# A routed expert kernel whose head is reordered: loads in one queue, weights in small staged pieces

## The chip, the cores and the metric

The kernel runs on one core of one Trainium2 chip. The metric is device microseconds of one execution; each figure is the median of several runs. A few names: PE is the matrix engine, DVE the vector engine, ACT the scalar engine, POOL the GpSimd engine, SP the sync engine, which here only issues transfers. "SPq" and "ACTq" in a row are transfers being issued by SP or ACT.

## The reference: what is computed

```python
# x: (8, 3584, 192), weight: (8, 7); 28672 tokens in all
w = softmax(weight)                                   # per head, over 7 taps
out[b,s,h,:] = sum_k w[h,k] * x_pad[b, s+k, h, :]     # causal conv, 8 heads of 24 channels
...
logits = x @ w_gate                                   # 8 experts
e_idx  = argmax(logits);  gate_w = softmax(logits)[e_idx]
eom    = sigmoid(x @ w_output_gate)
h  = relu(x[mask] @ w1[e])                            # 192 -> 1024
out[mask] = gate_w * eom[:, e] * (h @ w2[e])          # 1024 -> 192
```

## The kernel before, in words

The 28672 tokens are cut into 16 units of 1792 (16 blocks of 112). For each unit a generator `front(u)` does eight convolution matmuls, one for each head, against a banded matrix `band`; each result goes from PSUM to `cv`. Then come six groups of PE transposes (`tt`), the routing matmul (`pl`, `lt`), a transpose back (`pg`, `gb`), the argmax and softmax on DVE with two Exp instructions on ACT (`ex` and `ogs`), a running count for each expert (`pk`, `R`), and the scaled rows `xrow`. POOL then writes the unit's rows into a DRAM stream sorted by expert (`xcg_sorted`), in 16 indirect transfers. Two units make enough rows for the first four expert slots of 512 tokens. A slot is read back from the stream by two transposing transfers (`xa`, `xb`), multiplied by w1 (`first`) and w2 (`second`), and written out by four indirect transfers on POOL.

The program order on each engine is the order of the Python code, and every engine works through its own list in that order. The part up to the first slot is called the head here. It loads the units 0 and 1 (`load_x`), builds `band` from the conv weights by way of a DRAM scratch (`conv_band`), writes 512 rows of zeros at the start of each expert's part of the stream (the "guard"), loads all weights of 8 experts as fp32 and casts them to fp16 in the resident tile `wres` (`load_w`, `cast_w`), and runs `front(0)` and `front(1)`. The units 2 and 3 are loaded from inside `front(0)` and `front(1)`, after the eight convolutions of each, because `xt` has two buffers.

In the head before, ACT issues the band, the gate weights and the 32 guard transfers of 64 KB each. The weights of one expert come in four transfers into three staging buffers: `sa` (128x1024), `sb` (64x1024), and two halves of w2 (128x768). Two casts of an expert run on ACT and two on DVE. `evac` gives the copies from PSUM to the two engines in turn. One expert's casts and the next expert's loads follow each fifth step of the fronts:

```python
    while live:
        live = drain(f0, 1)
        emit_in(2)
        k += 1
        if k % 5 == 0:
            drain(wgen, 1)
```

At most eight transfers issued by SP and ACT together are under way at a time: there are eight completion semaphores for them, used in turn, and the issue of a transfer waits until the one eight places earlier has landed.

Of the kernel before, what the change touches and what calls it, by code (L numbers as in the profile page):

```python
# [11 lines left out]
FP16 = mybir.dt.float16  # L12
FP32 = mybir.dt.float32
# [8 lines left out]
def kernel(  # L22
# [10 lines left out]
    nc = tc.nc  # L33

    B, S, D = x.shape
    H, KW = weight.shape
    E = moe_w1.shape[0]
    F = moe_w1.shape[2]
# [3 lines left out]
    BT = 112  # L42
# [6 lines left out]
    TT = 512  # L49
    CAP = TT + N  # L50
    FCH = F // 128
    RW = 256
    IDC = 192
    ZW = 2 * BT + PADL + 2
    WE = F + F + FCH * D
    BIG = float(1 << 30)

    x_nd = x.rearrange("b s d -> (b s) d")
    xcg = nc.dram_tensor("xcg_sorted", (E * CAP, RW), FP16, kind="Internal").ap()
    z_dram = nc.dram_tensor("conv_band", (H, ZW), FP32, kind="Internal").ap()  # L60

    const = ctx.enter_context(tc.tile_pool(name="const", bufs=1))
    wst = ctx.enter_context(tc.tile_pool(name="wst", bufs=3))
    px = ctx.enter_context(tc.tile_pool(name="px", bufs=2))
    pcv = ctx.enter_context(tc.tile_pool(name="pcv", bufs=2))
    pct = ctx.enter_context(tc.tile_pool(name="pct", bufs=1))
# [11 lines left out]
    def load_x(u):  # L78
        xt = px.tile([128, NB, D], FP32, tag="xt", name="xt")
        t0 = u * UT  # L80

        def src(c0, nblk, q0, q1):
            return bass.AP(tensor=x_nd.tensor,
                           offset=x_nd.offset + (t0 + c0 * BT - PADL + q0) * D,
                           ap=[[D, q1 - q0], [BT * D, nblk], [1, D]])
        c0 = 0
        if u % UPB == 0:
            c0 = 1
            nc.vector.memset(xt[0:PADL, 0:1, :], 0.0)
            nc.sync.dma_start(xt[PADL:KI, 0:1, :], src(0, 1, PADL, KI))  # L90
        nc.sync.dma_start(xt[0:BT, c0:NB, :], src(c0, NB - c0, 0, BT))
        nc.sync.dma_start(xt[BT:KI, c0:NB, :], src(c0, NB - c0, BT, KI))
        return xt


    zt = const.tile([H, ZW], FP32)
    nc.vector.memset(zt, 0.0)
    cw = const.tile([H, KW], FP32)
    nc.sync.dma_start(cw, weight)
    xts = {0: load_x(0)}  # L100
    xts[1] = load_x(1)
    cmx = const.tile([H, 1], FP32)
    nc.vector.tensor_reduce(out=cmx, in_=cw, axis=AX.X, op=ALU.max)
    nc.vector.tensor_scalar(out=cw, in0=cw, scalar1=cmx, scalar2=None, op0=ALU.subtract)
# [3 lines left out]
    nc.vector.reciprocal(out=csm, in_=csm)  # L108
    nc.vector.tensor_scalar(out=zt[:, BT - 1:BT - 1 + KW], in0=cw, scalar1=csm,
                            scalar2=None, op0=ALU.mult)  # L110
    nc.scalar.dma_start(out=z_dram, in_=zt)
    band = const.tile([128, H, BT], FP32)
    for p0, p1 in ((0, BT), (BT, KI)):
        nc.scalar.dma_start(band[p0:p1],
                            bass.AP(tensor=z_dram.tensor, offset=z_dram.offset + p0,
                                    ap=[[1, p1 - p0], [ZW, H], [1, BT]]))


    wg = const.tile([128, 4, 32], FP32)
    nc.vector.memset(wg, 0.0)  # L120
    for i, (p0, p1, d0) in enumerate([(0, 128, 0), (0, 64, 128), (64, 128, 0), (0, 128, 64)]):
        nc.scalar.dma_start(wg[p0:p1, i, 0:E], moe_w_gate[d0:d0 + p1 - p0, :])
        nc.scalar.dma_start(wg[p0:p1, i, E:2 * E], moe_w_output_gate[d0:d0 + p1 - p0, :])


    ones_t = const.tile([128, 128], FP32)
# [48 lines left out]
    NXR = 3  # L175
    xrows = [const.tile([128, NB, RW], FP16, name=f"xrow{i}") for i in range(NXR)]
    for xr in xrows:
        nc.gpsimd.memset(xr[:, :, IDC:RW], 0.0)
        nc.vector.tensor_copy(out=xr[:, :, IDC + 1], in_=idlf)


# [1 line left out]
    for m in msks:  # L183
        nc.vector.memset(m, 0.0)


    zrow = const.tile([128, RW], FP16)
    nc.vector.memset(zrow, 0.0)


    wres = const.tile([128, E * WE], FP16)
    nc.gpsimd.memset(
        bass.AP(tensor=wres.tensor, offset=wres[64:65, F:F + 1].offset,
                ap=[[wres.ap[0][0], 64], [WE, E], [1, F]]), 0.0)

    def load_w(e):
        sa = wst.tile([128, F], FP32, tag="w", name="sa")
        nc.sync.dma_start(sa, moe_w1[e, 0:128, :])
        sb = wst.tile([128, F], FP32, tag="w", name="sb")
        nc.sync.dma_start(sb[0:64], moe_w1[e, 128:D, :])  # L200
        w2v = moe_w2[e].rearrange("(p c) d -> p c d", c=FCH)
        s2 = []
        for i in range(2):
            t = wst.tile([128, F], FP32, tag="w", name="s2")
            nc.sync.dma_start(t[:, 0:4 * D].rearrange("p (c d) -> p c d", d=D),
                              w2v[:, 4 * i:4 * i + 4, :])
            s2.append(t)
        return sa, sb, s2

    def cast_w(e, st):  # L210
        sa, sb, s2 = st
        o = e * WE
        nc.scalar.copy(out=wres[:, o:o + F].rearrange("p (c j) -> p c j", c=FCH),
                       in_=sa.rearrange("p (j c) -> p c j", c=FCH))
        nc.vector.tensor_copy(
            out=wres[0:64, o + F:o + 2 * F].rearrange("p (c j) -> p c j", c=FCH),
            in_=sb[0:64].rearrange("p (j c) -> p c j", c=FCH))
        nc.scalar.copy(out=wres[:, o + 2 * F:o + 2 * F + 4 * D], in_=s2[0][:, 0:4 * D])
        nc.vector.tensor_copy(out=wres[:, o + 2 * F + 4 * D:o + WE], in_=s2[1][:, 0:4 * D])

    sync_flip = [0]

    def evac(o, i):
        sync_flip[0] ^= 1
        if sync_flip[0]:
            nc.scalar.copy(out=o, in_=i)  # L226
        else:
            nc.vector.tensor_copy(out=o, in_=i)  # L228


    def front(u):
# [14 lines left out]
        for g in range(6):  # L246
            pt = ps_f.tile([128, 512], FP32, tag="pf", name="pt")
            for j in range(4):
                m, i = (g // 3) * 4 + j, g % 3
# [6 lines left out]
        pl = ps_f.tile([128, 512], FP32, tag="pf", name="pl")  # L256
# [4 lines left out]
                                 tt[:, g // 2 + i, (g % 2) * 4 * BT:(g % 2 + 1) * 4 * BT],  # L261
                                 start=(i == 0), stop=(i == 1), tile_position=(0, 32 * g))
        lt = pct.tile([128, 4 * BT], FP32, tag="lt", name="lt")
        nc.scalar.copy(out=lt, in_=pl[:, 0:4 * BT])
        yield
        pg = ps_f.tile([128, 512], FP32, tag="pf", name="pg")
        for j in range(4):
# [5 lines left out]
            out=gb[0:BT],  # L273
            in_=pg[0:BT].rearrange("p (k e) -> p k e", e=32)[:, :, 0:16])
# [12 lines left out]
            out=sc[P], in0=dl[P], scalar=0.0,  # L287
# [43 lines left out]
        xr = xrows[u % NXR]  # L331
# [5 lines left out]
        for g in range(4):  # L337
            nc.vector.tensor_tensor(  # L338
                out=xrv[P, g // 2, g % 2, :, 0:D], in0=cvv[P, g // 2, g % 2],
# [15 lines left out]
    def emit_in(n=1):  # L355
        while n and pend:
            if last[0] == "in":
                nc.gpsimd.nop()
            pend.popleft()()
            last[0] = "in"  # L360
            n -= 1
# [4 lines left out]
    def nodep(i, group, others):  # L366
        inst = i.ins if hasattr(i, "ins") else i
        for o in others:
            tc.declare_no_dep(inst, group=o, reason="distinct rows of the stream or output")
        tc.add_to_no_dep_group(group, inst)  # L370
# [5 lines left out]
    def plan_half(hf, nm):  # L376
# [18 lines left out]
        iu = pr.tile([128, EH, 4], U32, tag=f"iu{nm}", name="iu", bufs=3)  # L395
        nc.vector.tensor_scalar(out=iu, in0=iv, scalar1=BIG, scalar2=None, op0=ALU.mult)
        return [(e0 + i, bu[0:1, i:i + 1], iu[:, i, :]) for i in range(EH)]
# [19 lines left out]
    def w_at(off):  # L417
        return lambda o, n: wres[:, off + o:off + o + n]
# [64 lines left out]


    for e in range(E):
        for g in range(TT // 128):
            i = nc.scalar.dma_start(out=xcg[e * CAP + g * 128:e * CAP + (g + 1) * 128, :],
                                    in_=zrow)
            nodep(i, "guard", ())

    def drain(g, n=None):
        k = 0
        while n is None or k < n:
            try:
                next(g)
            except StopIteration:
                return False
            k += 1
        return True

    def chain(*gs):
        for g in gs:
            yield from g

    staged = {0: load_w(0)}

    def weights():
        for e in range(E):
            cast_w(e, staged.pop(e))
            if e + 1 < E:  # L510
                staged[e + 1] = load_w(e + 1)
            yield

    f0 = chain(front(0), front(1))
    wgen = weights()
    live = True
    k = 0
    while live:
        live = drain(f0, 1)
        emit_in(2)  # L520
        k += 1
        if k % 5 == 0:
            drain(wgen, 1)
    drain(wgen)
    emit_in(len(pend))

    prev = None
    for u in range(1, NU):
        todo = []
# [9 lines left out]
        for e, inv, xab in todo:  # L539
            s = Slot(xab, w_at(e * WE), inv)  # L540
            for q in range(4):
# [30 lines left out]
    with tc.For_i(0, rn, 1):  # L572
# [9 lines left out]
        sel = pr.tile([128, 1], U32, tag="sel", name="sel")  # L582
        nc.vector.tensor_scalar(out=sel, in0=om, scalar1=-float(WE), scalar2=float(E * WE),
                                op0=ALU.mult, op1=ALU.add)
# [16 lines left out]
        iv1 = pr.tile([128, 4], FP32, tag="iv1", name="iv1")  # L601
        nc.vector.tensor_scalar(out=iv1, in0=rowf, scalar1=tk1, scalar2=BIG,
                                op0=ALU.is_lt, op1=ALU.mult)
# [39 lines left out]
```

## Time and profile before

| | |
|---|---|
| median of 3 runs | 858.84 us (858.24 to 859.68) |
| the profiled execution, its time | 857.44 us |
| its span in the profile | 855.7 us |
| first expert matmul | 149.03 us |
| mean granted TensorE clock | 0.904 |
| busy: PE, DVE, ACT, POOL | 622.6, 334.0, 345.7, 523.7 us |

The span is the time from the first to the last recorded instruction; the execution's own time is 1.7 us longer. Busy shares are a mean over a head, in which the engines mostly wait, and a long main part that repeats for each unit.

### The profile page before, as it was taken

Reading aid. Unit: us, or ns where it says so; the run is one execution under the profiler, and the core shown is the slowest. Engines: PE = TensorE matmul, PEld = TensorE weight load, DVE = VectorE, ACT = ScalarE, POOL = GpSimd, SP = SyncE. Lnnn points to the kernel's source line nnn. Section 1 sums busy time; section 2 is a strip of 40 time slices with the busy share of each in tenths; the row PEclk is TensorE's granted clock in tenths of the full one; section 3 lists DMA queues with packets and bytes.
Section 4 is the critical chain, followed back from the end, with each engine's and each line's share of the span. In section 5 each row is a group of like instructions: output and inputs, shape, how many; then the busy total and the mean of one; then the engine's idle time right before and its main releaser. Section 6 shows DMA issues by size and latency. Waiting matters only on the chain. (4 is left out here: it accounts for less than half of the span.)

```text
span 855.7 us, 12810 instructions
## 1 busy us (share of the span) xinstructions
PE 622.6 (73%) x4612; PEld 397.9 (46%) x4612; DVE 334.0 (39%) x843; ACT 345.7 (40%) x503; POOL 523.7 (61%) x529
## 2 busy tenths in 40 slices
PE   1343610878098898989898989797979898669963
PEld 0121300435056565656555656464656555446641
DVE  6025340355035445362626253535353535112230
ACT  0133310325035454545444545454544544346631
POOL 4003415004775777777777777777777777777751
PEclk9975555889589999999999999999999999979987
DMA  7586741421263444444444445363632323244110
GB/s 163 162 200 185 215 102 51 105 68 31 62 156 102 124 106 126 113 118 117 119 109 131 106 126 139 101 140 95 147 90 77 84 78 91 70 108 124 59 38 6
DMA packets 132695, 92.93 MB, mean 109 GB/s; under 512 B 83379, under 2 KB 121428, under 8 KB 132631
## 3 DMA queue, kind: packets, MB, share of 16 engines
q1 hardware_dynamic: 105472, 52.81, 26.2%
q0 software_dynamic: 20672, 36.75, 14.6%
q10 hardware_dynamic: 6486, 2.55, 1.2%
q8 instruction: 36, 0.59, 0.3%
q14 instruction: 29, 0.23, 0.1%
HBM read 36.19 MB, written 42.34 MB: 92 GB/s over the span
## 5 line engine op out<-in xcount | busy, mean ns | idle before, releaser
L471 POOL DMA_INDIRECT out_dram<-y,oi x260 | 262.1, 1008 | 153.9 <-issue 71.4
L349 POOL DMA_INDIRECT xcg_sorted<-xrow,du x256 | 251.0, 980 | 165.8 <-DVE xrow L338 89.0
L442 ACT ACTIVATE ht<-pp 128x1024 f16<-128x1024 f32 x195 | 199.5, 1024 | 216.6 <-PE pp L436 192.8
L434 PE MATMUL pp<-xa,wres 128*128 128x512 f16 x520 | 201.1, 387 | 90.8 <-DMA xa<-xcg_sorted 64.7
L453 PE MATMUL pyt<-wres,ht 128*128 128x192 f16 (+1 forms) x2080 | 220.7, 249 | 22.4 <-DVE ht L440 22.4
L453 PEld LDWEIGHTS <-ht 128*128 128x128 f16 x2080 | 180.7, 99 | 82.5 <-DVE ht L440 25.7
L436 PE MATMUL pp<-xb,wres 128*128 128x512 f16 x520 | 200.9, 386 | 2.3 <-DMA xb<-xcg_sorted 2.3
L236 PE MATMUL pc<-xt,band 118*112 118x384 f32 x256 | 110.5, 560 | 46.8 <-DMA wg<-in_moe_w_gate_dram 18.1
L464 ACT COPY y<-pyt 128x384 f32<-128x384 f32 x130 | 62.1, 478 | 104.3 <-PE pyt L453 49.7
L436 PEld LDWEIGHTS <-wres 128*128 128x128 f16 (+1 forms) x520 | 51.4, 99 | 107.0 <-issue 77.1
L440 DVE TENSOR_SCALAR ht<-pp 128x1024 f16<-128x1024 f32 x65 | 79.4, 1221 | 46.5 <-PE pp L436 45.1
L228 DVE COPY cv<-pc 112x384 f32<-112x384 f32 x64 | 35.5, 556 | 146.0 <-PE pc L236 145.9
L236 PEld LDWEIGHTS pc<-xt,band 118*112 118x112 f32 x256 | 47.6, 199 | 85.9 <-ACT cv L226 24.9
L434 PEld LDWEIGHTS <-wres 128*128 128x128 f16 (+1 forms) x520 | 51.2, 98 | 64.7 <-DMA xa<-xcg_sorted 21.1
L467 DVE CAST oi<-pyt 128x4 uint32<-128x4 f32 x65 | 10.4, 160 | 180.9 <-ACT y L464 169.5
L226 ACT COPY cv<-pc 112x384 f32<-112x384 f32 x64 | 30.3, 476 | 76.8 <-PE pc L236 42.8
L250 PE MATMUL pt<-identf,cv 112*128 112x112 f32 x384 | 49.7, 273 | 12.4 <-ACT tt L226 6.6
L338 DVE TENSOR_TENSOR xrow<-cv,gs 112x768 f16<-112x768 f32 x64 | 58.3, 954 | 0.0
L250 PEld LDWEIGHTS pt<-identf,cv 112*128 112x128 f32 x384 | 41.9, 147 | 24.7 <-ACT tt L226 10.6
L228 DVE COPY tt<-pt 128x448 f32<-128x448 f32 x48 | 29.7, 621 | 34.3 <-PE pt L250 34.3
L226 ACT COPY tt<-pt 128x448 f32<-128x448 f32 x48 | 25.5, 530 | 32.4 <-PE pt L250 32.4
L259 PE MATMUL pl<-tt,wg 128*32 128x448 f32 x256 | 32.2, 596 | 2.0 <-ACT tt L226 1.0
(101 smaller groups left out, 284.2 us busy)
## 6 DMA issues: line engine op xcount, KB each, us to landing
xt<-in_x_dram SPq DMA_DIRECT2D x8, 1344.0 KB
xt<-in_x_dram SPq DMA_DIRECT2D x8, 1260.0 KB
s<-in_moe_w_dram SPq DMA_DIRECT2D x16, 384.0 KB
out_dram<-y,oi POOLq DMA_INDIRECT x260
sa<-in_moe_w_dram SPq DMA_DIRECT2D x8, 512.0 KB
xcg_sorted<-xrow,du POOLq DMA_INDIRECT x256
xcg_sorted<-zrow ACTq DMA_DIRECT2D x32, 64.0 KB
sb<-in_moe_w_dram SPq DMA_DIRECT2D x8, 256.0 KB
```

The source lines that it names most:

```text
L228: nc.vector.tensor_copy(out=o, in_=i)
L236: nc.tensor.matmul(pc[0:BT, 0:NB * GH], band[0:KI, h, :], xt[0:KI, :, h * GH:(h + 1) * GH], start=True, stop=True)
L250: nc.tensor.matmul(pt[:, j * BT:(j + 1) * BT], cvf[0:BT, m * 2 * D + i * 128:m * 2 * D + (i + 1) * 128], identf[0:BT, 0:BT], is_transpose= ...
L338: nc.vector.tensor_tensor(out=xrv[P, g // 2, g % 2, :, 0:D], in0=cvv[P, g // 2, g % 2], in1=gs[P, g:NB:4].unsqueeze(2).to_broadcast([BT, 4 ...
L349: i = nc.gpsimd.indirect_dma_start(out=xcg, out_offset=bass.IndirectOffsetOnAxis(ap=du[0:BT, kc(c):kc(c) + 1], axis=0), in_=xr[0:BT, c, :] ...
L434: nc.tensor.matmul(pp[:, j, :], self.w(fc * 128, 128), self.xa, start=True, stop=False)
L436: nc.tensor.matmul(pp[:, j, :], self.w(F + fc * 128, 128), self.xb, start=False, stop=True)
L440: nc.vector.tensor_relu(out=ht, in_=pp)
L442: nc.scalar.activation(out=ht, in_=pp, func=AF.Relu)
L453: nc.tensor.matmul(self.pp[:, o:o + D], self.ht[fc // 2][:, fc % 2, q * 128:(q + 1) * 128], self.w(2 * F + fc * D, D), start=(fc == 0 and ...
L464: nc.scalar.copy(out=self.y[:, q - 1:q + 1, :], in_=self.pp[:, 0:2 * D].rearrange("p (g d) -> p g d", d=D))
L471: i = nc.gpsimd.indirect_dma_start(out=out, out_offset=bass.IndirectOffsetOnAxis(ap=self.oi[:, j:j + 1], axis=0), in_=self.y[:, j, :], in_ ...
```

## The change

The same data is computed. Six things differ, all ahead of the main part but one:

- On SP's queue the order is now: unit 0, the conv scratch and the band, the gate weights, unit 1, the guard, then weights. ACT issues one transfer only, the conv weights.
- The guard is 8 transfers of 256 KB, with four stream rows for each partition, on SP.
- The weights come in 48 pieces of 256 KB (six for each expert) into five staging buffers; a new piece is loaded whenever one has been cast. All casts are on ACT: two of 128x512 and two of 64x512 with a strided read, three of 128x512 that are contiguous, for each expert.
- Each step of the fronts is followed by one piece's cast, in place of an expert's casts each fifth step.
- While the head lasts (`fill[0]`), every copy from PSUM is on DVE; afterwards they alternate again. `lt` now counts among the copies that alternate.
- The clears of `xrow` and `wres` move from POOL to DVE; those of `wres` cover the same bytes.

```diff
-    nc.sync.dma_start(cw, weight)
+    nc.scalar.dma_start(cw, weight)
     xts = {0: load_x(0)}
-    xts[1] = load_x(1)
...
-    nc.scalar.dma_start(out=z_dram, in_=zt)
+    nc.sync.dma_start(out=z_dram, in_=zt)
...
-        nc.scalar.dma_start(band[p0:p1],
+        nc.sync.dma_start(band[p0:p1],
...
+    xts[1] = load_x(1)
...
-        nc.gpsimd.memset(xr[:, :, IDC:RW], 0.0)
+        nc.vector.memset(xr[:, :, IDC + 2:RW], 0.0)
...
+    def load_w(e, i):
+
+        t = wst.tile([128, FH], FP32, tag="w", name="ws")
+        if i < 2:
+            nc.sync.dma_start(t, moe_w1[e, 0:128, i * FH:(i + 1) * FH])
+        elif i == 2:
+            for k in range(2):
+                nc.sync.dma_start(t[64 * k:64 * k + 64],
+                                  moe_w1[e, 128:D, k * FH:(k + 1) * FH])
+        else:
+            w2v = moe_w2[e].rearrange("(p c) d -> p (c d)", c=FCH)
+            nc.sync.dma_start(t, w2v[:, (i - 3) * FH:(i - 2) * FH])
+        return t
...
     def evac(o, i):
         sync_flip[0] ^= 1
-        if sync_flip[0]:
+        if sync_flip[0] and not fill[0]:
             nc.scalar.copy(out=o, in_=i)
...
-        nc.scalar.copy(out=lt, in_=pl[:, 0:4 * BT])
+        evac(lt, pl[:, 0:4 * BT])
...
-        for g in range(TT // 128):
-            i = nc.scalar.dma_start(out=xcg[e * CAP + g * 128:e * CAP + (g + 1) * 128, :],
-                                    in_=zrow)
-            nodep(i, "guard", ())
+        i = nc.sync.dma_start(
+            out=xcg[e * CAP:e * CAP + TT, :].rearrange("(p g) w -> p (g w)", g=GR), in_=zrow)
+        nodep(i, "guard", ())
...
     def weights():
-        for e in range(E):
-            cast_w(e, staged.pop(e))
-            if e + 1 < E:
-                staged[e + 1] = load_w(e + 1)
+        todo = [(e, i) for e in range(E) for i in range(NWP)]
+        ld = deque()
+        for k, (e, i) in enumerate(todo):
+            while len(ld) < NWST and k + len(ld) < len(todo):
+                ld.append(load_w(*todo[k + len(ld)]))
+            cast_w(e, ld.popleft(), i)
             yield
...
-        k += 1
-        if k % 5 == 0:
-            drain(wgen, 1)
+        drain(wgen, 1)
```

ACT before, from its last gate-weight transfer to the first Exp of unit 0 (`zrow` is the guard's source, `cv`, `tt` and `lt` are copies from PSUM, `sa` and `s` are staged weights):

```order
L123 DMA wg<-in_moe_w_output_gate_dram 128x8
L487 DMA xcg_sorted<-zrow 128x256 x32
L226 COPY cv<-pc 112x16x24 x3
L213 CAST wres<-sa 128x1024
L218 CAST wres<-s_216 128x768
L226 COPY cv<-pc 112x16x24
L226 COPY tt<-pt 128x448
L213 CAST wres<-sa 128x1024
L218 CAST wres<-s_244 128x768
```

ACT with the change, from its first weight cast to the two Exps of unit 0 (`ws` is a staged piece):

```order
L220 CAST wres<-ws 128x8x64 x2
L225 CAST wres<-ws 64x8x64 x2
L230 CAST wres<-ws 128x512 x3
L220 CAST wres<-ws 128x8x64 x2
L225 CAST wres<-ws 64x8x64 x2
L230 CAST wres<-ws 128x512 x3
L220 CAST wres<-ws 128x8x64 x2
L225 CAST wres<-ws 64x8x64 x2
L230 CAST wres<-ws 128x512
L298 ACTIVATE ex<-dl 112x128
L230 CAST wres<-ws 128x512
L323 ACTIVATE ogs<-ogs 112x16
```

The guard transfers and the copies from PSUM have left ACT. Ahead of unit 0's `ex` now stand the casts of 17 pieces, and ahead of unit 1's `ex`, by the same count further down the list, those of 40.

SP with the change, from the gate weights to the third expert's first pieces:

```order
L123 DMA wg<-in_moe_w_output_gate_dram 128x8
L92 DMA xt<-in_x_dram 112x16x192
L93 DMA xt<-in_x_dram 6x16x192
L500 DMA xcg_sorted<-zrow 128x1024 x8
L206 DMA ws<-in_moe_w_dram 128x512 x2
L209 DMA ws<-in_moe_w_dram 64x512 x2
L213 DMA ws<-in_moe_w_dram 128x512 x3
L206 DMA ws<-in_moe_w_dram 128x512 x2
L209 DMA ws<-in_moe_w_dram 64x512 x2
L213 DMA ws<-in_moe_w_dram 128x512 x3
L91 DMA xt<-in_x_dram 112x192
L92 DMA xt<-in_x_dram 112x15x192
```

The weights stand behind unit 1 and the whole guard, and unit 2 is requested after 12 pieces (unit 3, by the same list, after 36). Before, SP's first weight load came right after unit 1, and the guard went out beside it on ACT's queue.

DVE with the change, from the clear of the guard's source to unit 0's first wait on an Exp (`sm` reads `ex`):

```order
L191 MEMSET zrow 128x512
L195 MEMSET wres 64x8x512
L242 COPY cv<-pc 112x16x24 x8
L90 MEMSET xt 6x192
L242 COPY tt<-pt 128x448 x6
L242 COPY lt<-pl 128x448
L286 COPY gb<-pg 112x256
L292 TENSOR_REDUCE mx<-gb 112x16
...
L322 TENSOR_REDUCE ogs<-og 112x16
L325 TENSOR_REDUCE sm<-ex 112x16
```

No weight cast stands between these any more; before, each unit's copies had four to six of DVE's weight casts among them.

## Rows read from the trace of the kernel before

**Rows 1.** Busy time by stretch: PE, PEld, DVE, ACT, POOL, clock, DMA share, GB/s

```profile
0.00:149.00 149.00, 43.40 (x154) 19.84 (x155) 49.63 (x108) 31.75 (x38) 43.88 (x45) 0.70 0.60 154
149.00:235.00 86.00, 51.43 (x327) 29.31 (x327) 31.52 (x83) 23.63 (x38) 26.66 (x28) 0.82 0.27 68
235.00:835.00 600.00, 521.42 (x4088) 344.93 (x4087) 251.29 (x649) 287.41 (x423) 449.20 (x453) 0.97 0.42 107
```

**Rows 2.** Timeline, end of the head: start, duration, engine, line, instruction, [idle before]

```profile
120.10 0.28 DVE L311 TENSOR_REDUCE sm<-ex 112x16 f32<-112x128 f32 x1
...
124.47 1.40 POOL L349 DMA_INDIRECT xcg_sorted<-xrow,du  x1 [25.62 <-DVE xrow L338]
...
144.11 0.94 POOL L349 DMA_INDIRECT xcg_sorted<-xrow,du  x1 [0.30 <-issue]
...
149.03 0.59 PE L434 MATMUL pp<-xa,wres 128*128 128x512 f16 x1 [36.84 <-DMA xa<-xcg_sorted]
...
200.12 1.00 POOL L471 DMA_INDIRECT out_dram<-y,oi  x1 [55.07 <-ACT ht L442]
```

**Rows 3.** Timeline of ACT and its issues, around the guard

```profile
19.69 17.04 ACTq L487 DMA_DIRECT2D xcg_sorted<-zrow  x32
36.77 0.86 ACT L226 COPY cv<-pc 112x384 f32<-112x384 f32 x2 [33.96 <-DMA xcg_sorted<-zrow]
```

**Rows 4.** Groups by line and shape, first 150 us: busy, mean ns, idle before

```profile
L213 ACT CAST wres<-sa 128x1024 f16<-128x1024 f32 x8 | 16.3, 2036 | 15.6 <-DMA sa<-in_moe_w_dram 15.6
...
L218 ACT CAST wres<-s 128x768 f16<-128x768 f32 x8 | 6.6, 831 | 0.2 <-DMA s<-in_moe_w_dram 0.2
L219 DVE CAST wres<-s 128x768 f16<-128x768 f32 x8 | 4.5, 563 | 26.1 <-DMA s<-in_moe_w_dram 26.1
L228 DVE COPY cv<-pc 112x384 f32<-112x384 f32 x8 | 4.4, 552 | 24.5 <-PE pc L236 24.4
```

**Rows 5.** Timeline: first casts of three experts, and the last expert's

```profile
71.14 2.03 ACT L213 CAST wres<-sa 128x1024 f16<-128x1024 f32 x1
...
98.88 2.06 ACT L213 CAST wres<-sa 128x1024 f16<-128x1024 f32 x1
...
114.00 2.03 ACT L213 CAST wres<-sa 128x1024 f16<-128x1024 f32 x1 [3.72 <-DMA sa<-in_moe_w_dram]
...
119.10 0.56 DVE L219 CAST wres<-s 128x768 f16<-128x768 f32 x1 [3.07 <-DMA s<-in_moe_w_dram]
```

**Rows 6.** Busy time by stretch, columns as in rows 1

```profile
2.00:17.00 15.00, 0.00 (x0) 0.00 (x0) 12.44 (x25) 0.29 (x2) 10.39 (x9) 1.00 1.03 216
...
32.00:37.00 5.00, 0.00 (x0) 0.00 (x0) 0.00 (x0) 0.23 (x1) 0.00 (x0) 1.00 0.47 141
...
94.00:97.00 3.00, 0.31 (x2) 0.34 (x3) 1.03 (x2) 0.00 (x0) 2.21 (x3) 0.58 1.02 368
104.00:109.00 5.00, 4.15 (x12) 0.87 (x6) 1.23 (x3) 0.53 (x1) 0.00 (x0) 0.50 1.13 261
```

**Rows 7.** Timeline, start: band, unit 1's second transfer, first convolution

```profile
11.54 0.84 ACTq L114 DMA_DIRECT2D band<-conv_band  x2
...
17.81 0.28 SPq L92 DMA_DIRECT2D xt<-in_x_dram  x1
...
18.12 2.87 PE L236 MATMUL pc<-xt,band 118*112 118x384 f32 x4 [18.12 <-DMA wg<-in_moe_w_gate_dram]
```

**Rows 8.** Timeline of PE in unit 1's front (a conv matmul counts twice)

```profile
86.82 4.18 PE L236 MATMUL pc<-xt,band 118*112 118x384 f32 x6 [1.65 <-DVE cv L228]
...
96.69 4.43 PE L250 MATMUL pt<-identf,cv 112*128 112x112 f32 x20 [5.21 <-DVE cv L228]
102.16 4.89 PE L259 MATMUL pl<-tt,wg 128*32 128x448 f32 x16 [1.03 <-ACT tt L226]
```

**Rows 9.** Timeline: the clear on POOL, and a DVE instruction beside it

```profile
7.30 6.92 POOL L192 MEMSET wres<- 64x8192 f16 x1
7.31 6.94 DVE L143 TENSOR_SCALAR rev<-eoff 128x8 f32<-128x8 f32 x1
```

More of the change, by code (lines that the diff above doesn't have):

```diff
@@ L55 @@
     WE = F + F + FCH * D
+    NWST = 5
     BIG = float(1 << 30)
@@ L62 @@
     const = ctx.enter_context(tc.tile_pool(name="const", bufs=1))
-    wst = ctx.enter_context(tc.tile_pool(name="wst", bufs=3))
+    wst = ctx.enter_context(tc.tile_pool(name="wst", bufs=NWST))
     px = ctx.enter_context(tc.tile_pool(name="px", bufs=2))
@@ L121 @@
     for i, (p0, p1, d0) in enumerate([(0, 128, 0), (0, 64, 128), (64, 128, 0), (0, 128, 64)]):
-        nc.scalar.dma_start(wg[p0:p1, i, 0:E], moe_w_gate[d0:d0 + p1 - p0, :])
-        nc.scalar.dma_start(wg[p0:p1, i, E:2 * E], moe_w_output_gate[d0:d0 + p1 - p0, :])
+        nc.sync.dma_start(wg[p0:p1, i, 0:E], moe_w_gate[d0:d0 + p1 - p0, :])
+        nc.sync.dma_start(wg[p0:p1, i, E:2 * E], moe_w_output_gate[d0:d0 + p1 - p0, :])
+    xts[1] = load_x(1)
     ones_t = const.tile([128, 128], FP32)
@@ L184 @@
         nc.vector.memset(m, 0.0)
-    zrow = const.tile([128, RW], FP16)
+    GR = TT // 128
+    zrow = const.tile([128, GR * RW], FP16)
     nc.vector.memset(zrow, 0.0)
     wres = const.tile([128, E * WE], FP16)
-    nc.gpsimd.memset(
+    nc.vector.memset(
         bass.AP(tensor=wres.tensor, offset=wres[64:65, F:F + 1].offset,
                 ap=[[wres.ap[0][0], 64], [WE, E], [1, F]]), 0.0)
[L196 to L208, printed above, removed]
@@ L210, in cast_w @@
-    def cast_w(e, st):
-        sa, sb, s2 = st
-        o = e * WE
[L213 to L219, printed above, removed]
+    FH = F // 2
@@ new lines @@
+    NWP = 6
+    def load_w(e, i):
[10 more added lines that the diff above has]
+        return t
@@ new lines, in cast_w @@
+    def cast_w(e, t, i):
+        o = e * WE
+        if i < 2:
+            nc.scalar.copy(
+                out=wres[:, o:o + F].rearrange("p (c j) -> p c j", c=FCH)[:, :, i * 64:i * 64 + 64],
+                in_=t.rearrange("p (j c) -> p c j", c=FCH))
+        elif i == 2:
+            for k in range(2):
+                nc.scalar.copy(
+                    out=wres[0:64, o + F:o + 2 * F].rearrange(
+                        "p (c j) -> p c j", c=FCH)[:, :, k * 64:k * 64 + 64],
+                    in_=t[64 * k:64 * k + 64].rearrange("p (j c) -> p c j", c=FCH))
+        else:
+            nc.scalar.copy(out=wres[:, o + 2 * F + (i - 3) * FH:o + 2 * F + (i - 2) * FH],
+                           in_=t)
@@ L221 @@
     sync_flip = [0]
+    fill = [True]
     def evac(o, i):
         sync_flip[0] ^= 1
-        if sync_flip[0]:
+        if sync_flip[0] and not fill[0]:
             nc.scalar.copy(out=o, in_=i)
@@ L503, in chain @@
             yield from g
-    staged = {0: load_w(0)}
     def weights():
-        for e in range(E):
-            cast_w(e, staged.pop(e))
-            if e + 1 < E:
-                staged[e + 1] = load_w(e + 1)
+        todo = [(e, i) for e in range(E) for i in range(NWP)]
[4 more added lines that the diff above has]
+            cast_w(e, ld.popleft(), i)
             yield
@@ L516 @@
     live = True
-    k = 0
     while live:
@@ L520 @@
         emit_in(2)
-        k += 1
-        if k % 5 == 0:
-            drain(wgen, 1)
+        drain(wgen, 1)
     drain(wgen)
     emit_in(len(pend))
+    fill[0] = False
     prev = None
```

## The prediction

> **What bounds the kernel now.** I read the busy time by stretch first, because the page's shares mix two stages. In the main part, 235 to 835 us, POOL issues 453 indirect transfers in 600 us [rows 1]. When nothing holds it back, a scatter takes 0.94 us with 0.30 us of issue ahead [rows 2]. 453 times 1.24 us are 562 of the 600 us, so POOL paces the main part, with PE (521 us busy) close behind. In the first 149 us no engine is busy for even 50 us and the DMA engines stand at a share of 0.60 [rows 1]: this is waiting. The change touches the head, so the question is when the first expert matmul starts. Now it starts at 149.03, released by the read of the sorted stream [rows 2]. All later work hangs on it: POOL idles 55 us until the first output at 200.12 and then runs nearly without a pause. The span behind the first expert matmul is 855.7 - 149.0 = 706.7 us. The same instructions fill it after the change, so I carry it over unchanged.
>
> Next I followed the chain backwards. From `sm` of unit 1 at 120.10 to the first expert matmul it takes 28.9 us: 4.4 us of DVE work, 20.6 us for 16 scatters, 4 us to read back [rows 2]. This tail stays. What makes `sm` late? Three things, in the order of time. ACT issues 32 guard transfers for 17.04 us and so comes to its first copy from PSUM only at 36.77, after 34 us of idling [rows 3]; the convolution could start at 18.12 [rows 7]. Then weight casts stand between the fronts' copies on both engines and wait for transfers: 15.6 us before the `sa` casts on ACT, 26.1 us before the second w2 half on DVE [rows 4]; the latter has to wait for a staging buffer first. At the end, DVE's cast at 119.10 waits 3.07 us and `sm` is right behind it [rows 5, 2]. An expert's weights take 9.25 us: three of them from 71.14 to 98.88 [rows 5], with the DMA engines at rest for part of it.
>
> **The change, part by part.**
>
> *Start of the front.* Before, the scratch had landed by 11.54, when the band is issued, with units 0 and 1 around it, and the band at about 17.8 with unit 1 beside it [rows 7]. Now only unit 0 (1.45 MB) is ahead. At 216 GB/s [rows 6] it takes 6.7 us from 2.0, so the scratch lands near 10. The band alone takes between 3 us (0.42 MB at that rate and a landing delay of about 1) and the 6.3 us it took in company; I take 5, near the upper end since its rows are short. First convolution near 15.5 instead of 18.1. The gain itself is hidden, as seen below.
>
> *Start of the weights.* Unit 1 is issued after the gate weights, near 16; 1.45 MB at 216 GB/s and a landing delay end at 24. The guard is 2.1 MB. Before, it ran at 141 GB/s with the DMA engines at a share of 0.47 [rows 6], that is 300 GB/s if it fills them, or 141 at worst: 7 or 15 us. The eight transfers now are 256 KB each and need only 8 issues, so I take 7: 31. The first weight piece is queued behind, landing near 33 (28 if everything here runs at 300 GB/s, 39 with the slow guard). Before, weights were issued from 21 on, so this edit by itself is a loss of several us.
>
> *Pace of the weights.* A piece is 262 KB. The DMA engines at their best moved 368 GB/s of weights [rows 6], 0.71 us for a piece. ACT's casts: 1024 strided elements take 2.04 us, 768 contiguous ones 0.83 [rows 4]. So a strided 512 takes 1.02 and a contiguous one 0.55; an expert's 4 + 3 casts take 5.7 us, 0.96 for a piece, the lower bound. The upper bound is the pace of before, 9.25 / 6 = 1.54. One transfer alone is slow: after ACT freed the buffer at 116.03, 393 KB were there for the cast 3.07 us later [rows 5]. A piece of 262 KB has 0.13 MB less to move and should take about 2.7 us; with the cast that is 3.7 us for a buffer's round, and five buffers give 0.73 us a piece if transfers overlap. All three terms (0.71, 0.96, 0.73) lie below 1.0 but share their time unevenly, so I take 1.1, near the cast bound.
>
> *What waits for the weights.* The Exp of unit 0 stands on ACT behind the casts of 17 pieces, that of unit 1 behind 40; DVE waits for each at `sm`. Units 2 and 3 are loaded between the pieces, at 1.45 MB and 261 GB/s [rows 6] 5.6 us, say 6 each. Unit 1's `ex` can thus start at 33 + 40 x 1.1 + 12 + 1 (last cast) = 90.
>
> *The other side of that wait.* Unit 0's `ex` comes at 33 + 17 x 1.1 + 6 + 1 = 59; its own front was through long before (15.5 plus some 25 us of the steps below), so the earlier start buys nothing. Then DVE needs 7 us to the last `xrow`, near 66. Unit 1's front follows on DVE and PE: six convolutions not done ahead at 1.39 us, six transposition groups at about 1.1, the routing matmul 4.9 [rows 8], copies and first reductions about 3: 23 us. The copies are all on DVE, at 0.55 us [rows 4] below PE's 1.39, so giving up ACT's half costs nothing. This side is ready at 89. The two sides meet; `ex` runs at 90, and with the 0.3 us of `ex` and the 28.9 us tail the first expert matmul starts at 119.5.
>
> *Edits that cost nothing.* DVE now clears `wres`. POOL took 6.9 us for the same bytes, and a small DVE instruction beside it lasted as long [rows 9]. On DVE I bound it by 0 and 6.9 us; all set-up is done before the first convolution at 15.5, or a microsecond after it, and unit 0's front has 17 us to spare before its Exp. Moving transfers from ACT to SP costs SP eight guard issues and a few more; SP has no other work. `lt` on DVE in every second unit of the main part adds about 0.6 us to an engine that is 42% busy there [rows 1].
>
> *The sum.* 149.0 - 119.5 = 29.5 us less, of which I keep 29. From the profiled execution 857.4 - 29 = 828.4; the median of before is 1.4 above that execution, so **830 us**.
>
> The Trainium skill ("DMA: Bandwidth & Descriptors", section "Rules for kernel authors") speaks against this change: for full bandwidth it wants at least 1 MiB in a transfer, and the same page ("Anatomy of one DMA") gives about 2.0 us fixed cost plus the bytes at 436 GB/s, as an estimate 2.6 us for 262 KB. If pieces did not overlap at all that would be 2.6 us a piece and about 890 us in all. The trace agrees on the latency of a lone transfer (3.07 us for 393 KB, where the formula gives 2.9), and disagrees on the consequence, since 368 GB/s were moved by transfers of 256 to 512 KB [rows 5, 6].
>
> **The rivals.** With s for the landing of the first piece and p for the pace, the weights' side gives a first expert matmul at s + 40 p + 12 + 1 + 29.2.
>
> *Weights at their old pace.* p = 1.54: 137 us, 12 us gained, 847. For it: that pace was measured, and the same DMA engines carry the units and scatters. Against: the old pace contained a wait for a buffer in each expert, which five buffers and a cast after every step remove.
>
> *More than forecast.* s = 28 and p = 0.96: the fronts' side then decides, near 81, first matmul near 110.5; 820 us. For it: DMA bursts of 368 GB/s. Against: ACT would have to cast without a pause.
>
> *Slower.* Every front now waits on ACT for weights, with 17 and 40 pieces ahead. If small transfers hardly overlap, the head grows: it is slower from p = 1.85 on, and at the 2.7 us of a lone piece the first matmul comes at 183, 34 us later, 893. For it: a lone transfer is that slow, and the old guard, in 64 KB transfers, moved 141 GB/s, just 1.86 us for each 262 KB. Against: that guard took 0.53 us of issue for each 64 KB, so issue explains it.
>
> *No change.* The head is shorter, but the main part does not follow, since something other than the first expert matmul times POOL's start. I find no such row: POOL's 55 us of idling ends with the first slot's output. 859.
>
> **How the numbers follow.** Forecast (first matmul between 113 and 126): 0.56. More: 0.17. Old pace: 0.17. Slower: 0.06. No change: 0.04. The range takes the forecast and the two neighbours, 820 to 847. A measurement of this kernel can tell about 0.2% (1.7 us) from no change. Faster by more than that 0.90, within it 0.04, slower 0.06.
>
> **What would show it.** In the changed profile: the first expert matmul near 120 and 707 us behind it; ACT in the head with casts alone, about 1.1 us apart from piece to piece between 33 and 100; DVE waiting some 17 us at unit 0's `sm` for ACT's `ex`; unit 1's `sm` near 90; the first convolution near 15.5. I am wrong if pieces land 1.5 us apart or slower, if the first piece lands after 40, if SP stands at unit 3's load for a convolution that isn't done (all weights behind it would stand too), or if the time behind the first expert matmul is not 707 us.

## The result, and the profile after

The changed kernel takes **830.22 us** (median of 4 runs, 829.0 to 831.14), the kernel before 858.54 (4 runs): a ratio of 0.9675, 95% interval 0.9645 to 0.9705. On chip C of the experiments the same pair gave 830.09 against 857.32, ratio 0.968 (0.965 to 0.971).

First the busy time by stretch of the changed kernel, columns as in [rows 1]:

```profile
0.00:120.00 120.00, 30.73 (x154) 14.91 (x155) 42.72 (x112) 49.80 (x62) 33.02 (x41) 0.69 0.69 191
120.00:829.00 709.00, 582.82 (x4458) 379.08 (x4457) 287.28 (x742) 311.51 (x458) 481.02 (x484) 0.95 0.39 99
```

Up to the first expert matmul the span is now 120 us where it was 149 [rows 1, 2]. The DMA engines are busier there (0.69 against 0.60), and every engine still mostly waits. Behind it lie 709 us.

Then rows from the timeline of the changed kernel's head: start, duration, engine, line, instruction, number, [idle before <- what ended it]:

```profile
9.19 3.47 DVE L195 MEMSET wres<- 64x4096 uint32 x1 [0.91 <-issue]
10.18 0.81 SPq L114 DMA_DIRECT2D band<-conv_band  x2
13.92 8.45 PE L250 MATMUL pc<-xt,band 118*112 118x384 f32 x16 [13.92 <-DMA wg<-in_moe_w_gate_dram]
16.91 8.10 SPq L500 DMA_DIRECT2D xcg_sorted<-zrow  x8
25.06 0.93 SPq L206 DMA_DIRECT2D ws<-in_moe_w_dram  x2
30.95 2.13 ACT L220 CAST wres<-ws 128x512 f16<-128x512 f32 x2 [28.00 <-DMA ws<-in_moe_w_dram]
32.99 2.23 ACT L225 CAST wres<-ws 64x512 f16<-64x512 f32 x2
35.24 1.66 ACT L230 CAST wres<-ws 128x512 f16<-128x512 f32 x3
...
39.11 0.42 SPq L92 DMA_DIRECT2D xt<-in_x_dram  x1
...
40.24 2.44 SPq L206 DMA_DIRECT2D ws<-in_moe_w_dram  x2
...
52.12 2.11 ACT L220 CAST wres<-ws 128x512 f16<-128x512 f32 x2 [9.28 <-DMA ws<-in_moe_w_dram]
...
56.91 0.30 ACT L298 ACTIVATE ex<-dl 112x128 f32<-112x128 f32 x1
57.25 0.29 DVE L325 TENSOR_REDUCE sm<-ex 112x16 f32<-112x128 f32 x1 [25.00 <-ACT ex L298]
...
63.15 6.20 PE L250 MATMUL pc<-xt,band 118*112 118x384 f32 x12 [3.48 <-DVE cv L242]
69.35 3.89 PE L264 MATMUL pt<-identf,cv 112*128 112x112 f32 x24
...
72.16 0.42 SPq L92 DMA_DIRECT2D xt<-in_x_dram  x1
...
73.31 1.71 PE L273 MATMUL pl<-tt,wg 128*32 128x448 f32 x16
...
74.98 1.17 SPq L213 DMA_DIRECT2D ws<-in_moe_w_dram  x1
...
77.26 0.29 DVE L294 TENSOR_TENSOR dl<-gb,mx 112x128 f32<-112x128 f32 x1
...
85.51 0.62 ACT L230 CAST wres<-ws 128x512 f16<-128x512 f32 x1 [6.78 <-DMA ws<-in_moe_w_dram]
...
90.69 0.31 ACT L298 ACTIVATE ex<-dl 112x128 f32<-112x128 f32 x1
...
91.03 0.29 DVE L325 TENSOR_REDUCE sm<-ex 112x16 f32<-112x128 f32 x1 [11.86 <-ACT ex L298]
...
95.42 1.40 POOL L363 DMA_INDIRECT xcg_sorted<-xrow,du  x1 [14.52 <-DVE xrow L352]
...
115.07 0.94 POOL L363 DMA_INDIRECT xcg_sorted<-xrow,du  x1 [0.30 <-issue]
...
117.43 1.22 SPq L425 DMA_TRANSPOSE xa<-xcg_sorted  x1
...
120.02 0.59 PE L448 MATMUL pp<-xa,wres 128*128 128x512 f16 x1 [40.67 <-DMA xa<-xcg_sorted]
```

Read it by the two DVE rows on `sm`. Both wait for ACT's `ex`, 25.00 us in unit 0 and 11.86 us in unit 1. ACT comes to each `ex` straight out of a weight cast: no idle time is shown ahead of the rows at 56.91 and 90.69. The input of unit 1's `ex` (`dl`) was there from 77.6 on. So the weights' side alone sets the end of the head. Inside it stand two stalls of 9.28 and 6.78 us, at the casts whose pieces (issued at 40.24 and 74.98) lie behind the loads of units 2 and 3 in SP's queue. From `sm` of unit 1 to the first expert matmul it is 29.0 us, where it was 28.9.

One count that the prediction used was off by one. In the list of ACT's instructions 16 pieces stand ahead of unit 0's `ex`, and in the trace 39 ahead of unit 1's; 17 and 40 are the counts ahead of `ogs`, behind each `ex`. Unit 3 is requested after 35 pieces, not 36, and the second stall is at the 36th. Paces below are worked out with 39.

### The profile page after: what moved, and what is told of

Its sections match the earlier page's. It is cut to its first block, busy times and chain, and to the rows that moved or that the text cites. A ratio compares the mean times of both kernels' runs of the same rounds, so it can differ in the third digit from the quotient of the medians.

```text
span 829.4 us, 12842 instructions
## 1 busy us (share of the span) xinstructions
PE 613.5 (74%) x4612; PEld 394.0 (48%) x4612; DVE 330.0 (40%) x854; ACT 361.3 (44%) x520; POOL 514.0 (62%) x525
## 5 line engine op out<-in xcount | busy, mean ns | idle before, releaser
L250 PE MATMUL pc<-xt,band 118*112 118x384 f32 x256 | 105.8, 540 | 46.5 <-DVE R L333 24.4
L242 DVE COPY cv<-pc 112x384 f32<-112x384 f32 x72 | 40.0, 556 | 122.8 <-PE pc L250 122.5
L250 PEld LDWEIGHTS pc<-xt,band 118*112 118x112 f32 x256 | 45.8, 192 | 82.7 <-issue 43.8
L264 PE MATMUL pt<-identf,cv 112*128 112x112 f32 x384 | 47.5, 263 | 3.8 <-ACT tt L240 3.1
L264 PEld LDWEIGHTS pt<-identf,cv 112*128 112x128 f32 x384 | 40.1, 141 | 14.9 <-ACT tt L240 5.0
L242 DVE COPY tt<-pt 128x448 f32<-128x448 f32 x54 | 33.5, 621 | 32.3 <-PE pt L264 32.0
L240 ACT COPY cv<-pc 112x384 f32<-112x384 f32 x56 | 26.8, 478 | 43.1 <-PE pc L250 43.1
L220 ACT CAST wres<-ws 128x512 f16<-128x512 f32 x16 | 17.3, 1112 | 38.5 <-DMA ws<-in_moe_w_dram 38.5
L240 ACT COPY tt<-pt 128x448 f32<-128x448 f32 x42 | 22.3, 531 | 24.5 <-PE pt L264 24.5
```

Source lines behind the costliest of these rows:

```text
L250: nc.tensor.matmul(pc[0:BT, 0:NB * GH], band[0:KI, h, :], xt[0:KI, :, h * GH:(h + 1) * GH], start=True, stop=True)
L264: nc.tensor.matmul(pt[:, j * BT:(j + 1) * BT], cvf[0:BT, m * 2 * D + i * 128:m * 2 * D + (i + 1) * 128], identf[0:BT, 0:BT], is_transpose= ...
```

## The experiments

A kernel is compared only with others on its own chip, because two of the three chips of the experiments run all kernels, the one before too, about 30% longer (the last section shows it). On chip A the kernel before took 1124.17 us (median of 9 runs), on chip B 1123.66 (7), on chip C 857.32 (7). "Before" in a ratio is always that chip's.

**The guard alone, on the kernel before (chip A).** The guard leaves ACT's queue for SP's, in 16 transfers; nothing else changes.

```diff
...
-        for g in range(TT // 128):
-            i = nc.scalar.dma_start(out=xcg[e * CAP + g * 128:e * CAP + (g + 1) * 128, :],
-                                    in_=zrow)
+        for g in range(2):
+            o = e * CAP + g * 256
+            i = nc.sync.dma_start(
+                out=xcg[o:o + 256, :].rearrange("(p g) w -> p (g w)", g=GR), in_=zrow)
```

> The kernel before, with the guard alone moved from ACT to SP (16 transfers of 128 KB). My theory: the head is paced by the weights and their casts (9.25 us an expert before), so freeing ACT lets the chain of casts start some 10 us earlier and no more; first expert matmul near 139, time near 849. Rival: ACT's 34 us of idling behind the guard was the main cost, and its removal alone brings most of the gain: time near 835. Second rival: nothing, since the weights then stand behind the guard on SP: 858.

Measured: 1114.87 us, ratio 0.9925 (0.9896 to 0.9953), 9.3 us less; the first expert matmul came at 141.16. The guard's issues on ACT did hold up the head, but moving them is the smaller part.

**The guard back on ACT, in the changed kernel (chip A).**

```diff
...
-        i = nc.sync.dma_start(
-            out=xcg[e * CAP:e * CAP + TT, :].rearrange("(p g) w -> p (g w)", g=GR), in_=zrow)
...
+        for g in range(TT // 128):
+            i = nc.scalar.dma_start(out=xcg[e * CAP + g * 128:e * CAP + (g + 1) * 128, :],
+                                    in_=zrow)
...
```

> The changed kernel with the guard put back on ACT in 32 transfers of 64 KB. My theory: with no copies from PSUM on ACT in the head, the guard there delays nobody; the first weights land near 31 to 36 as before, first expert matmul 119 to 124, time 829 to 835. Rival (the guard on ACT costs in itself): 15 us or more back, 845.

Measured: 1102.88 us, ratio 0.9808 (0.9773 to 0.9843), 21.3 us less than before; first cast at 34.04, first expert matmul at 124.97. The changed kernel itself ran on chip B and not on chip A; there it gained 21.8 us. Set side by side across the two chips, the guard's 32 issues on ACT cost little with all copies on DVE: SP issues the first piece at 30.95 where the changed kernel does at 25.06, the first cast comes 3 us later, and the gains differ by half a microsecond. The edits overlap. Either one takes the guard out of the way of the copies.

**The changed kernel on chip B, and three copies of it with one edit each.** The control, the changed kernel as it is:

> The changed kernel itself, as a control beside the others of this group: the last group ran on a chip on which the kernel before took 1124 us. Where the kernel before takes 858 us, 830; on a chip like the last one, 1124 less 28, that is 1096. In both, the same gain in us, since the change touches the head alone.

Measured: 1101.9 us, ratio 0.9814 (0.9772 to 0.9856); first expert matmul at 121.39.

Three staging buffers for five:

```diff
-    NWST = 5
+    NWST = 3
```

> The changed kernel with three staging buffers for the pieces in place of five. My theory (a buffer's round of some 3.7 us divided by the buffers bounds the pace): 1.23 us a piece in place of 1.09, 40 pieces ahead of unit 1's Exp, 5 to 7 us more than the changed kernel. Rival (the pace is bound by ACT's casts or the DMA engines): no difference.

Measured: 1107.68 us, 5.8 more than the control; first expert matmul at 129.24, 7.9 later. Unit 1's `ex` starts at 99.94, the first cast at 31.24. Less the two long stalls (8.29 and 7.30 us) that leaves 53.1 us for 39 pieces, 1.36 us each, against 1.13 with the control's five buffers. The pace does hang on the number of transfers under way.

The copies from PSUM in turn on both engines in the head, as before the change:

```diff
-        if sync_flip[0] and not fill[0]:
+        if sync_flip[0]:
```

> The changed kernel with the copies from PSUM alternating between ACT and DVE in the head too. My theory: ACT is the pace-setter between the two unit loads, and 15 copies of 0.5 us stand among its casts ahead of unit 1's Exp: 6 to 10 us more than the changed kernel. Rival (DVE is the tighter one in the head, so ACT's half helps): as the changed kernel or faster.

Measured: 1102.37 us, ratio 0.9806 (0.976 to 0.9851): the expected 6 to 10 us did not come. In the trace ACT's copies take 0.47 to 0.54 us each, and some of them fall into the first stall; unit 1's `ex` starts at 93.78, 3.3 us later than in the control, and the first expert matmul at 124.89, 3.5 later. The two profiled executions differ by 3.9 us, the medians by 0.5, with runs of each spread over 4 us. What this edit is worth lies between nothing and 4 us. Unit 1's `ex` waits 0.33 us for `dl` here: on chip B pauses of PE (last section) make the front as late as the weights, so the run doesn't show what the copies cost on ACT's side alone.

**Fewer casts ahead of the Exps.** Half the pace in the fronts (chip A): one piece for every second step, the rest behind unit 1's front.

```diff
...
-        drain(wgen, 1)
+        k += 1
+        if k % 2 == 0:
+            drain(wgen, 1)
```

> The changed kernel with one piece cast after each second step of the fronts, the rest cast behind the fronts, so that 8 and 19 pieces stand ahead of the two Exps in place of 17 and 40. My theory (the Exps behind the casts set the end of the head, the fronts themselves are ready at 77.6): unit 1's sm near 65, scatters done near 90, the read of the stream then issued behind the last weight load near 95, first expert matmul 97 to 100, time 808 to 811. Rival (the fronts, the scatters or the transfers in total set the end): 826 to 830.

Units 2 and 3 loaded behind the weights (chip A):

```diff
-        if u + 2 < NU:
+        if 2 <= u and u + 2 < NU:
...
     drain(wgen)
+    xts[2] = load_x(2)
+    xts[3] = load_x(3)
```

> The changed kernel with units 2 and 3 loaded behind the weights and no longer from inside the fronts. ACT's casts stood 9.3 and 6.8 us at these two loads. My theory: the Exp of unit 1 comes 16 us earlier, first expert matmul near 104, time near 814. Rival (the transfers share the DMA engines anyway, or unit 1's front becomes the later side): a gain under 5 us, 826 or more; and if the main part's first fronts then wait for units 2 and 3, the gain is given back there.

Half the pace as above, and the last four experts' 24 pieces cast between the steps of the first slots (chip B; `done` counts the pieces cast in the fronts):

```diff
...
-    drain(wgen)
...
+    drain(wgen, EH * NWP - done)
...
+                drain(wgen, 2)
...
```

> The changed kernel with one piece after each second step of the fronts, and only the weights of experts 0 to 3 (24 pieces), which the first four slots use, ahead of the first slot; the other 24 pieces are loaded and cast between the first slots' steps. My theory: the wait for the weights ends the head, so the first expert matmul comes near 90 (30 us earlier than in the changed kernel), and the main part's first stage takes the 24 casts at a cost of a few us: 25 us less than the changed kernel, near 805 where that takes 830. Rival (the pieces now delay the first slots by as much as they no longer delay the head): no gain over the changed kernel.

Measured on chips A and B: half pace 1086.35 us, ratio 0.967 (0.9629 to 0.971), first expert matmul at 108.10; late units 1093.2, ratio 0.9739 (0.9699 to 0.978), matmul at 114.60; half pace with deferred pieces 1087.92, ratio 0.9696 (0.9653 to 0.9739), 14 below its control, matmul at 104.95. All three ratios are lower than the changed kernel's on chip B (0.9814), though the interval of the late units just touches its own. But the matmul came 8 to 11 us later than expected of the first two, and 15 later than the 90 expected of the third, because unit 1's front was late: PE paused inside it for 4 to 7 us at a time. That left it open whether the front or the weights are the limit, so the edits ran again on a third chip, C.

**The same on chip C.** The control:

> The changed kernel as it is, to stand beside the other three on their chip. If the kernel before takes 858 us there, this one takes 830 with the first expert matmul at 120; if it takes 1124, this one takes 1102 with it at 121.

Measured: 830.09 us, first expert matmul at 119.88.

Half pace:

> One weight piece every second step of the fronts, once more. Theory: the weights' side alone sets the end of the head and unit 1's front is ready at 77.6, so unit 1's Exp moves to 78, the first expert matmul to 107, and the time 13 us below the changed kernel's. Rival: PE has gaps inside unit 1's front whatever stands beside it, as it had in the first run of this edit (Exp at 74, first expert matmul at 108, but only 16 us below the kernel it was cut from by the time); then the matmul comes at 108 again. What tells them apart is whether the matmuls of unit 1's front run without idle time.

Measured: **809.28 us**, ratio 0.9443 (0.9412 to 0.9473), 20.8 below the control. First expert matmul at 98.93, 8 us earlier than expected. Its timeline, columns as above:

```profile
39.29 0.30 ACT L298 ACTIVATE ex<-dl 112x128 f32<-112x128 f32 x1
...
60.17 0.29 DVE L294 TENSOR_TENSOR dl<-gb,mx 112x128 f32<-112x128 f32 x1
...
60.49 0.31 ACT L298 ACTIVATE ex<-dl 112x128 f32<-112x128 f32 x1
...
69.14 0.18 DVE L341 SCALAR_TENSOR_TENSOR gs<-ogs,sm 112x16 f32<-112x16 f32 x1 [3.82 <-ACT ogs L323]
...
90.52 0.94 POOL L363 DMA_INDIRECT xcg_sorted<-xrow,du  x1 [0.30 <-issue]
...
92.93 1.49 SPq L213 DMA_DIRECT2D ws<-in_moe_w_dram  x3
95.36 1.22 SPq L425 DMA_TRANSPOSE xa<-xcg_sorted  x1
```

I had taken 77.6 as a fixed time at which unit 1's front is ready. It isn't: that front starts when unit 0's `ex` has run, and with `ex` at 39.29 for 56.91 it is ready at 60.5, 17 us earlier. Its transposes ran with gaps of at most 0.27 us; the pauses of chip A are absent. Two new waits take part of it back. `ogs` now stands behind a cast that waits for unit 3's load (3.82 us on DVE), and the first `xa` stands behind weights on SP: it is issued 3.9 us after the last scatter's end, where the changed kernel takes 1.4.

Late units:

> Units 2 and 3 loaded behind all the weights, once more. Theory: the 16 us that ACT waited for the two unit loads go; the weights' side is ready at 75, unit 1's front at 77.6 sets the end, first expert matmul at 107, 13 us below the changed kernel. Rival: units 2 and 3 are then missed by their own fronts, which gives part of it back: first output on POOL early, but PE waiting for unit 2 and only 8 us gained.

Measured: 813.49 us, ratio 0.9494 (0.9463 to 0.9525), 16.6 below the control, first expert matmul 16.4 earlier, at 103.48:

```profile
47.90 0.30 ACT L298 ACTIVATE ex<-dl 112x128 f32<-112x128 f32 x1
...
74.19 0.31 ACT L298 ACTIVATE ex<-dl 112x128 f32<-112x128 f32 x1
74.53 0.29 DVE L325 TENSOR_REDUCE sm<-ex 112x16 f32<-112x128 f32 x1 [3.46 <-ACT ex L298]
...
106.24 6.96 PE L250 MATMUL pc<-xt,band 118*112 118x384 f32 x16
```

Both stalls of ACT are gone (those of the changed kernel on the chip of the result and on chip C add up to 16.1 and 16.7 us), and unit 2's convolutions at 106.24 start without waiting for their input. At their place the two unit loads cost as much as the stalls. The theory that the front then sets the end did not hold: `ex` at 74.19 again comes straight out of a cast, and `sm` waits 3.46 us for it.

Half pace, deferred pieces and late units together, with the other lines as in the edits above:

```diff
...
-    drain(wgen)
...
+    drain(wgen, EH * NWP - done)
+    xts[2] = load_x(2)
+    xts[3] = load_x(3)
...
```

> Half pace in the head, the last four experts' 24 pieces cast between the steps of the first slots, and units 2 and 3 loaded behind the pieces. Theory: unit 1's front sets the end already at half pace, so the late unit loads bring nothing more: first expert matmul at 105 to 107, 13 to 15 us below the changed kernel. Rival: the unit loads still stand in the way of the 24 pieces ahead of unit 1's Exp; then it is 5 us or more below the half-pace kernel.

Measured: **804.6 us**, ratio 0.939 (0.936 to 0.942), the fastest of all and 25.5 below the control. The first expert matmul comes at 90.89, 29.0 earlier than the control's; 3.5 us are given back behind it. The timeline, and then the busy time by stretch from the first expert matmul to the first output, of this kernel and of the changed one:

```profile
59.92 0.31 ACT L298 ACTIVATE ex<-dl 112x128 f32<-112x128 f32 x1 [8.15 <-DVE dl L294]
...
100.51 2.17 ACT L220 CAST wres<-ws 128x512 f16<-128x512 f32 x2
...
146.07 1.00 POOL L485 DMA_INDIRECT out_dram<-y,oi  x1 [59.41 <-ACT wres L220]
```

```profile
90.90:146.10 55.20, 40.73 (x232) 21.39 (x231) 26.97 (x77) 27.45 (x42) 0.03 (x1) 0.85 0.54 132
```

```profile
120.00:172.40 52.40, 39.90 (x232) 21.53 (x231) 26.96 (x77) 16.29 (x28) 0.04 (x1) 0.89 0.30 74
```

The matmul came 14 us earlier than the 105 expected, for the reason given under half pace: the front moves with unit 0's `ex`. Against the half-pace kernel it is 4.7 us less, close to what the rival asked; how much of that the late units bring and how much the deferred pieces, no run on chip C tells. Unit 1's `ex` waits 8.15 us for `dl` here: of the runs on chip C only this one has the front as the later side. The deferred casts are 11.2 us more of ACT's work in the first slots (27.45 against 16.29), and the stretch to the first output is 2.8 us longer, with a cast right ahead of it.

## Why the prediction was right

**First expert matmul at 119.5, and the time moves with it one for one.** It came at 120.02. On chip C the time followed it: 20.8 us for 20.9 (half pace), 16.6 for 16.4 (late units), 25.5 for 29.0 (deferred pieces, where ACT's extra work shows). The span behind it is 709.4 us where I carried 706.7 over; the 2.7 us more are not explained by any run. What each of the six edits brings to the 28.3 us is shown in part only: the guard alone brought 9.3 us on chip A, five buffers for three 5.8 on chip B, the copies 0 to 4 there; the small pieces with all casts on ACT never ran alone.

**Start of the front: 15.5.** It was 13.92: 3.7 us after the band's issue at 10.18, where it took 6.3 with unit 1 beside it. As I said, the gain is hidden.

**First piece lands near 33.** The first cast starts at 30.95. The guard's eight issues took SP 8.10 us, and the weights follow at 25.06.

**Pace 1.1 us a piece.** From 30.95 to 90.69 are 59.7 us for 39 pieces; without the two stalls 43.7, so 1.12. With three buffers it was 1.36. Two strided casts in a row take 2.13 us and three contiguous ones 1.66, near the 1.02 and 0.55 each that I worked out.

**Two unit loads, 6 us each.** This term was too small: the stalls are 9.28 and 6.78, 16.1 us in place of 12. The busy time by stretch of the changed kernel, at the first pieces, in the first stall, in unit 1's front, and in the second stall:

```profile
25.00:31.00 6.00, 3.66 (x28) 1.97 (x28) 3.79 (x9) 0.05 (x1) 0.00 (x0) 1.00 1.06 355
...
43.00:52.00 9.00, 0.00 (x0) 0.00 (x0) 0.00 (x0) 0.00 (x0) 0.00 (x0) 0.50 1.09 219
...
64.00:79.00 15.00, 11.73 (x65) 5.76 (x64) 10.00 (x21) 12.13 (x14) 11.34 (x13) 0.91 0.90 260
...
79.00:85.50 6.50, 0.35 (x13) 0.28 (x10) 0.17 (x1) 0.00 (x0) 1.60 (x2) 0.62 1.10 286
```

What those stretches moved shows in the sizes of the packets. The rows are the changed kernel from 43 to 52 us, the same from 43 to 45, and the kernel before from 104 to 109, where I took the 261 GB/s of a unit [rows 6]. A unit travels in rows of 768 bytes, a piece in rows of 2 KB:

```profile
DMA packets 1867, 1.97 MB, mean 219 GB/s; under 512 B 87, under 2 KB 1394, under 8 KB 1867
...
DMA packets 658, 0.51 MB, mean 253 GB/s; under 512 B 0, under 2 KB 658, under 8 KB 658
...
DMA packets 1657, 1.31 MB, mean 261 GB/s; under 512 B 16, under 2 KB 1643, under 8 KB 1657
```

In the first stall no engine works and the DMA engines are full (1.09), yet they move only 219 GB/s, where the end of the guard and the first pieces, both in rows of 2 KB, moved 355 at the same share. About half of the 1.97 MB are rows of unit 2, the other half later pieces. Alone the unit's rows moved at 253 GB/s, so the rate that I had taken was right. What I left out is the company: the piece that ACT waits for lies behind the unit and shares the engines with the pieces behind it too. With the units out of the way the pace is the same (44.1 us for 39 pieces in the late-units run, 1.13), so a unit costs the weights' side some 8 us, where its own rate gives 5.7. Why the mixed stretch is slower than either kind alone is not shown.

**Unit 0's Exp at 59, unit 1's at 90.** 56.91 and 90.69. The first piece came 2 us early, the 1 us for a last cast was not needed, and the unit loads took 4 us more; these largely cancel. The sum was better than its terms, and that was luck. DVE's wait at unit 0's `sm` is 25.0 us where I said 17: unit 0's front was through at 32, not near 40.

**"The two sides meet."** This step failed. I put the fronts' side at 89; it was ready at 77.6. I costed unit 1's front at 23 us from [rows 8] (with 1.1 us for a transposition group, where the row gives 0.89), where PE ran at a granted clock of 0.50 in the last part [rows 6] and stood between DVE's and ACT's weight casts. In the changed kernel nothing stands between the copies, and PE has 0.91 in this stretch (64 to 79 us, above), near its upper level of 2.4 GHz, where 0.50 is the lower one: six convolutions take 6.20 us, the transposes 3.89 and the routing matmul 1.71. The whole front takes some 15 us. It did not change the sum, because the weights' side sets the end, but it hid how much more there was to gain: 16 to 25 us by the runs on chip C.

**The clear of `wres` on DVE.** 3.47 us, inside the bounds of 0 and 6.9, and over at 12.7, ahead of the first convolution.

**The rivals.** The old pace (1.54) and the slower case (above 1.85) are excluded by 1.12, and "no change" by the runs on chip C, where the time follows the first expert matmul. "More than forecast" (820) asked for a first piece at 28 and a pace of 0.96; 30.95 and 1.12 were measured, and two stalls of ACT besides. ACT casting with only short pauses is what the late-units run made, and that gave 813.

The Trainium skill's rule in "DMA: Bandwidth & Descriptors", section "Rules for kernel authors", wants 1 MiB in a transfer; the trace disagrees on its consequence, since transfers of 256 KB (guard and pieces) moved 355 GB/s with several under way. The fixed cost of a transfer that the Trainium skill gives ("DMA: Bandwidth & Descriptors", section "Anatomy of one DMA") is stated there for transfers issued by POOL, and the pieces are issued by SP; taken over all the same, a piece is 2.6 us, an estimate, and with its cast 3.6 us of a buffer's round. The trace agrees with that in direction only: it would make 1.2 us a piece from three buffers and 0.7 from five, where 1.36 and 1.12 were measured.

## What to carry to other kernels

An in-order queue makes everything ahead of a small urgent instruction urgent: here two Exps of 0.3 us stood behind 16 and 39 weight casts, of which the first slots need 24. When two sides seem to meet, check whether one of them starts from the other; the front of unit 1 moved with unit 0's Exp, so shortening the weights' side paid twice. A large load in the middle of a queue of small ones can cost those behind it more than its own bytes take: here 8 us for each unit, where its own rate gives 5.7.

## What the hardware showed that I had not expected

The changed kernel takes 1102 us on chip B and 830 on the chip of the result and on chip C; the kernel before takes 1124 on chips A and B and 857 to 859 on the other two. PE's longest waits of the changed kernel on chip B (engine, line and name, what it waited for: us in total, times, longest) and two rows of its timeline there:

```profile
PE pp L448 <- ACT ht L456: 118.3, 26, 13.9
PE pp L448 <- issue: 55.7, 9, 8.8
PE pyt L467 <- issue: 38.2, 28, 2.3
```

```profile
75.96 1.01 PE L264 MATMUL pt<-identf,cv 112*128 112x112 f32 x4 [3.48 <-issue]
83.80 1.01 PE L264 MATMUL pt<-identf,cv 112*128 112x112 f32 x4 [6.83 <-issue]
```

On the chip of the result the same view reads:

```profile
PE pp L448 <- DMA xa<-xcg_sorted: 69.6, 3, 40.7
PE pp L448 <- ACT ht L456: 24.5, 10, 8.4
```

On chip B PE pauses for up to 8.8 us with nothing recorded that it waits for, and the mean granted clock of the span is 0.823 against 0.909. There is no such row for `pp` or `pyt` on the faster chips. It looks as if PE was not given its instructions in time, but that is only argued: the instruction queues moved the same 0.59 and 0.22 MB in both traces, and no run here tells what PE waited for, or why these chips differ. For the reader it means that a gain measured on one chip need not be that of another: the change is worth 28.3 and 27.2 us where PE does not pause, and 21.8 on chip B.
